# A gated blend of segment-recurrent and dilated attention: K's prepass in rounds of 16 chunks, more resident slices, other buffers and queues

## The chip, the cores and the metric

One Trainium2 chip, one NeuronCore of it. The metric is the device time of one execution of the whole program, in microseconds (us). The engines of the core are named as the profile names them: PE multiplies matrices (PEld loads its weights), DVE and ACT work on vectors, POOL is the general engine, SP only issues DMA transfers. SP, ACT and POOL each issue their transfers in their own program order; 16 DMA engines move the bytes.

## The reference

Activations and weights are bfloat16. With x of 2048 tokens by 640:

```python
g = sigmoid((x * gate_w).sum(-1))                # one gate per token
mem = mem0                                       # 8 x 640
for s in range(64):                              # segments of 32 tokens
    h = concat([mem, x[32*s:32*s+32]])           # 40 x 640
    q, k, v = h @ Wq, h @ Wk, h @ Wv             # 32 heads x 192 = 6144 columns each
    p = softmax(mask(q @ k.T * 192**-0.5))
    o = (p @ v) @ Wo                             # 40 x 640
    mem = o[:8]                                  # carried to the next segment
    a[32*s:32*s+32] = o[8:]
# branch B: 32 heads x 20, each token sees itself and 7 more, 2 apart
q, k, v = x @ wqkv
b = softmax_over_8(q[t] . k[t - 2*w] * 20**-0.5) v[t - 2*w] @ wo
out = g * a + (1 - g) * b
```

Only the 8 memory rows of a segment depend on the segment before. What the tokens' rows need of q, k and v does not, so some of it can be prepared for all 64 segments ahead.

## The kernel before

The program runs through these stages, in this order. The times are those of the profiled execution.

**Branch B, 0 to 190 us (`part_b`).** The tokens are cut into a short block (b = 0, 112 tokens, with an input tile of its own, `xT0`) and four blocks of 484. For each block, `proj(b, n, c)` makes one of five 128-row chunks of q (n = 0) or k (n = 1): five matmuls, a cast to a tile called `bqc` or `bkc` (DVE for q, and for k from block 2 on; ACT for k of blocks 0 and 1), and a store by SP into DRAM. Four tiles rotate under each of the two names, so a cast waits until the store of the cast four places earlier has landed. `load_qk(b)` then reads q and k of the block back in the layout the scores need (`bqT`, `bkT`: eight SP loads), `make_v` makes V, `gates` makes the gate values (it needs `gw_sb`, loaded from gate_w), `scores` and `values` do the attention by groups of heads. Finished rows go through DRAM into `OTc`, and `out_tile` multiplies them by wo, puts the result into a tile `bo` beside the gate, and stores it in `bsc_dram` with POOL; four `bo` tiles rotate.

The order on PE, ACT, DVE and SP is written out by hand within a `manual_schedule`: at its start `load_qk(0)`, two entries of a list of bulk loads (`fetch(2)`: xT of block 2 and gate_w), `make_v(0)`, the first projections of block 1, `gates(0)`. Then a planner deals projections, gates, V and out tiles to the steps of (block, group of heads) by cost and due step; one bulk load is issued per step for most steps. The bulk list holds what the later stages need: resident weight slices (`wres`), Q's columns of the prepass, `zTi`. After the last block the gate values are stored to `g_dram` and read back as a tile `gZ` of 128 x 4 by 16 small SP loads.

**The prepass, 190.7 to 352 us (`prepass`).** The first eight tokens' rows of all 64 segments (`zTi`, 640 x 512) are multiplied by Wq, Wk and Wv. For Q and K the result has 48 chunks of 128 columns each: five matmuls into one of eight PSUM banks, then a cast by ACT or DVE in turn into a tile `ZS` (128 x 64 segments x up to 192 values per segment), two of which rotate. A round is the chunks that share a `ZS`: 16 for Q, 24 for K. Each Q round is stored with one transfer of 2 MB by ACT; each K round with two, one of 128 values per segment (2 MB) and one of 64 (1 MB, runs of 128 bytes), into `zpk_dram`. The weight columns come from resident slices or, where a slice is not resident, through slots `wst` (POOL loads, 256 KB each, for K). V follows: for three column parts t and four groups of 128 rows, 20 matmuls and four casts into a tile `ZV` (three rotate), stored by ACT with 4 transfers each.

Beside that SP loads weight slices of part A into the space that is free: `load_late(0)` takes slices up to a bound `LATE0` (bytes per partition) while Q runs; `load_late(1)`, after the `ZS` tiles are gone, the rest, and `load_late(2)` the last seven after V. The order of the slices is q, k, v, oa, ob (parts of Wo).

**Part A, 352 us to the end.** A first segment on its own, a loop over the segments at some 18 us each (390 to 1500), and a tail. Each segment reads its prepared row of `zpk_dram` (`load_z`, and `load_vz` on POOL into `aVz`), and part of the weights is streamed from DRAM through `wst` slots by SP in every segment. L805 is its q and k matmul, L812 ACT's cast of that. Loop and tail are not touched by the diff.

The lines that the change and the prediction speak of: 143 and 141 (casts by DVE and ACT), 252 (V of B), 225 (gates), 271 and 275 (a projection's matmul and its store), 281 (`load_qk`), 347, 361, 367 and 369 (`bo`: gate copy, matmul, DVE part, store), 467 (the `gZ` loads), 526 (slice loads), 590 (K's columns), 612 and 624 (Q/K matmul and store), 638 and 646 (V matmul and store), 743 (`load_vz`).

Of the kernel before, what the change touches and what calls it, by code (L numbers as in the profile page):

```python
# [10 lines left out]
BF = mybir.dt.bfloat16  # L11
F32 = mybir.dt.float32
I32 = mybir.dt.int32

SLOTS = 7
N_EARLY = 15
N_EARLY2 = 12
N_LAST = 7
LATE0 = 41984
STREAM = [("q", 0, 1, 1), ("k", 0, 1, 1), ("k", 0, 3, 1), ("q", 1, 1, 0), ("k", 1, 0, 0), ("k", 1, 3, 1), ("q", 2, 2,  # L20
          0), ("k", 2, 0, 1), ("k", 2, 1, 1), ("k", 2, 4, 1), ("v", 0, 3, 1), ("v", 1, 1, 0), ("v", 1, 4, 1), ("v", 2,
          0, 1), ("v", 2, 3, 0), ("oa", 3, 1), ("oa", 4, 1), ("ob", 2, 0), ("oa", 7, 0), ("oa", 11, 0), ("ob", 6, 0)]
# [71 lines left out]
class _K:  # L94
# [59 lines left out]
    def part_b(self, outer):  # L154

        nc, tc, KC, S = self.nc, self.tc, self.KC, self.S
        NQ, HALO = 121, 14
# [4 lines left out]
        g_dram = self.dram.tile([4, 32, self.NT], F32, name="g_dram")  # L162
        self.xh_dram = self.laid["xh"]
        self.gZ = self.const.tile([128, 4], F32, name="gZ")
        self.pre_columns = {}
        with ExitStack() as ctx:
# [96 lines left out]
            def proj(b, n, c):  # L263
                nq, nu, c0 = shape_of(b)
                nt = nq * nu
                o0, nn = ((c0 + HALO, nt), (c0, nt + HALO))[n]
                if c == 0:
                    qk_dram[b, n] = self.dram.tile([640, nn], BF, name=f"b{'qk'[n]}_dram{b}")
                ps = bank(F32, "ps_bqk")
                for kc in range(KC):  # L270
                    nc.tensor.matmul(ps[:, 0:nn], lhsT=wqk[n][:, c, kc, :], rhs=(xT if b else xT0)[:, kc, o0:o0 + nn],
                                     start=(kc == 0), stop=(kc == KC - 1))
                t = wk.tile([128, BQ + HALO], BF, name="b" + "qk"[n] + "c", bufs=4)
                self.evac(t[:, 0:nn], ps[:, 0:nn], "dve" if n == 0 or b > 1 else "act")
                nc.sync.dma_start(qk_dram[b, n][128 * c:128 * c + 128], t[:, 0:nn])

# [66 lines left out]
            ot_dram = {}  # L343

            def out_tile(ti, padded=False):
                bo = io.tile([128, 4, 162], BF, name="bo", bufs=4)
                nc.gpsimd.tensor_copy(bo[:, :, 160:162].bitcast(F32),
                                      self.g_sb[:, ti:ti + 1].unsqueeze(1).to_broadcast([128, 4, 1]))
                for f in range(2):
# [26 lines left out]
                    proj(0, n, c)  # L376

            def columns(p):
                self.pre_columns[p] = self.get_columns("q", p)
# [53 lines left out]
            for i, (b, g) in enumerate(steps):  # L433
                work = plans[i]
                fill(work[:1])
                scores(b, g)
                fill(work[1:])
                if i > 0:
                    values(*steps[i - 1])
                if b + 1 < nb and g == 3:  # L440
                    load_qk(b + 1)
                if b > 0 and g == 1:
                    store_ot(b - 1, 0, 8)
                if b > 0 and g == 2:
# [17 lines left out]
            fill(rest)  # L462
            nc.vector.tensor_copy(last[:, :, o0:128], OTb[(nb - 1) % 2][:, 5:8, 0:128 - o0])
            nc.sync.dma_start(g_dram[:].rearrange("u t n -> (u t) n"), self.g_sb[:])
            for n in range(4):
                for q in range(4):
                    nc.sync.dma_start(self.gZ[32 * q:32 * q + 32, n:n + 1], g_dram[:, 24:32, 4 * n + q:4 * n + q + 1])
            fetch(len(bulk))
            order.close()
            for ti in (13, 14, 15, 12):  # L470
# [105 lines left out]
        self.nc.gpsimd.dma_start(t, self.wscr[key])  # L576
        return self.view(t, key)

    def get_columns(self, m, p):

        W = {"q": self.Wq, "k": self.Wk}[m].rearrange("(c p) f -> p c f", p=128)
        out = {}
        for x in range(2):
            for kc in range(self.KC):
                if (m, p, kc) in self.res_tiles:
                    t = self.res_tiles[m, p, kc][:, 1024 * x:1024 * x + 1024]
                else:
                    t = self.slots[self.slot_at % SLOTS]
                    self.slot_at += 1
                    (self.nc.sync if m == "q" else self.nc.gpsimd).dma_start(t[:], W[:, kc, 2048 * p + 1024 * x:2048 * p + 1024 * x + 1024])  # L590
                out.setdefault(kc, []).extend(t[:, f:f + 128] for f in range(0, 1024, 128))
        return out

    def prepass(self):
# [5 lines left out]
        zTi = self.zTi  # L600
        with tc.tile_pool(name="pre_zv", bufs=3, side="right", reuse_waits="tile") as zvp:
            with tc.tile_pool(name="pre_zs", bufs=2, reuse_waits="tile") as zp:
                for m in ("q", "k"):
                    n = 16 if m == "q" else 24
                    for c in range(48):
                        if c % n == 0:
                            ZS = zp.tile([128, nseg, 192], BF, name="ZS")
                        if c % 16 == 0:
                            sls = self.pre_columns[c // 16] if m == "q" else self.get_columns(m, c // 16)
                        ps = self.pst([128, NZ], F32, name="ps_pre")  # L610
                        for kc in range(KC):
                            nc.tensor.matmul(ps[:], lhsT=sls[kc][c % 16],
                                             rhs=zTi[:, kc, :], start=(kc == 0), stop=(kc == KC - 1))
                        zc = 8 * (c % 16) if m == "q" else 16 * (c % 12) + 8 * (c // 12 % 2)
                        self.evac(ZS[:, :, zc:zc + 8], ps[:].rearrange("p (i s) -> p s i", i=8))
                        if c % n == n - 1:
                            if m == "q":
                                zs = [(256 * (c // n) + 128, 0, 128)]
                            elif c < n:
                                zs = [(0, 0, 128), (256, 128, 64)]  # L620
                            else:
                                zs = [(320, 0, 64), (512, 64, 128)]
# [8 lines left out]
            for t in range(3):  # L631
                sls = [self.v_columns(t, kc) for kc in range(KC)]
                for st in range(NZ // 128):
# [9 lines left out]
                                  "dve" if (t, st) == (2, NZ // 128 - 1) else None)  # L643
                    for k in range(2 * st, 2 * st + 2):
                        for e, R, x, n in V_PIECES[t]:
                            nc.scalar.dma_start(self.zpk_dram[:, 8 * R + k:128:32, 768 + x:768 + x + n],
                                                ZV[64 * (k % 2):64 * (k % 2) + 64, :].rearrange(
                                                    "s (j e) -> s j e", j=4)[:, :, e:e + n])

    def working_tiles(self):  # L650

# [599 lines left out]
```

## Time and profile before

| | us |
|---|---|
| median of 3 runs | 1554.81 (1549.94 to 1559.15) |
| the profiled execution | 1561.53 |
| its span | 1559.8 |
| branch B | 0 to 190.7 |
| Q and K of the prepass | 190.7 to 242.5, 242.5 to 294.3 |
| V of the prepass | 294.3 to 352.1 |
| part A | 352.1 to 1559.8 |

| engine | busy us | share of the span |
|---|---|---|
| PE | 1460.0 | 94% |
| DVE | 815.2 | 52% |
| ACT | 642.5 | 41% |
| POOL | 204.8 | 13% |

All lines below come from one execution taken by the hardware profiler. A line of the timeline names the start, the time until the end of the last instruction of the group, the engine, the line of the program, the operation with out<-in, the number of instructions, and in brackets how long the engine stood idle before it and which instruction ended that. An engine's busy share says little by itself: the share is an average over stages with different limits.

### The profile page before, as it was taken

Reading aid. Unit: us, or ns where it says so; the run is one execution under the profiler, and the core shown is the slowest. Engines: PE = TensorE matmul, PEld = TensorE weight load, DVE = VectorE, ACT = ScalarE, POOL = GpSimd, SP = SyncE. Lnnn points to the kernel's source line nnn. Section 1 sums busy time; section 2 is a strip of 40 time slices with the busy share of each in tenths; the row PEclk is TensorE's granted clock in tenths of the full one; section 3 lists DMA queues with packets and bytes.
Section 4 is the critical chain, followed back from the end, with each engine's and each line's share of the span. In section 5 each row is a group of like instructions: output and inputs, shape, how many; then the busy total and the mean of one; then the engine's idle time right before and its main releaser. Section 6 shows DMA issues by size and latency. Waiting matters only on the chain. (4 is left out here: it accounts for less than half of the span.)

```text
span 1559.8 us, 90918 instructions
## 1 busy us (share of the span) xinstructions
PE 1460.0 (94%) x36746; PEld 818.7 (52%) x36746; DVE 815.2 (52%) x2246; ACT 642.5 (41%) x1673; POOL 204.8 (13%) x432
## 2 busy tenths in 40 slices
PE   6988799996899999999999999999999999999969
PEld 3444444433555555555555555555555555555547
DVE  2787433323555555555555555556555555555510
ACT  2588422222344434443444344434443444344430
POOL 0000201100111111111111111111111111111100
PEclk8999999998999999999999999999999999999979
DMA  6788686999899999999999999999999999999980
GB/s 188 193 210 218 187 272 154 222 269 281 279 330 322 318 325 325 330 325 329 330 326 322 325 323 330 324 326 332 318 318 327 334 325 321 322 332 325 303 189 16
DMA packets 374073, 446.29 MB, mean 286 GB/s; under 512 B 132504, under 2 KB 236488, under 8 KB 374008
## 3 DMA queue, kind: packets, MB, share of 16 engines
q1 hardware_dynamic: 272632, 395.77, 77.4%
q10 hardware_dynamic: 87824, 25.14, 7.2%
q0 software_dynamic: 13552, 24.47, 5.1%
q8 instruction: 46, 0.75, 0.2%
q14 instruction: 19, 0.16, 0.0%
HBM read 407.04 MB, written 38.20 MB: 285 GB/s over the span
## 5 line engine op out<-in xcount | busy, mean ns | idle before, releaser
L812 ACT CAST aP<-psx 128x512 bf16<-128x512 f32 x128 | 68.7, 589 | 362.5 <-PE psx L805 349.4
L967 PEld LDWEIGHTS <-aP 128*32 128x32 bf16 x6144 | 163.8, 96 | 66.2 <-ACT aP L946 18.5
L903 PE MATMUL psm<-wlate_v,aHa 128*32 128x512 bf16 x2048 | 186.9, 380 | 0.3 <-issue 0.3
L805 PEld LDWEIGHTS <-aHa 128*32 128x32 bf16 x4608 | 117.5, 96 | 122.5 <-issue 21.0
L967 PE MATMUL psm<-wlate_oa,aP 128*32 128x384 bf16 x2560 | 167.7, 329 | 0.0
L827 DVE STREAM_TRANSPOSE aK<-aP 128x512 bf16<-128x512 bf16 (+1 forms) x256 | 135.0, 547 | 7.4 <-ACT aP L812 1.1
L967 PE MATMUL psm<-wst,aP 128*32 128x384 bf16 (+1 forms) x896 | 121.5, 306 | 10.7 <-DMA wst<-in_slices_dram 10.7
L805 PE MATMUL psm<-wres_q,aHa 128*32 128x512 bf16 x1280 | 118.8, 381 | 11.0 <-ACT aK L812 4.7
L967 PE MATMUL psm<-wlate_ob,aP 128*32 128x256 bf16 x2688 | 126.1, 274 | 1.2 <-issue 1.2
L824 DVE STREAM_TRANSPOSE aP<-aP 128x512 bf16<-128x512 bf16 (+1 forms) x128 | 74.1, 579 | 87.4 <-ACT aP L812 87.4
L946 DVE CAST aP<-psx 128x128 bf16<-128x128 f32 (+2 forms) x192 | 75.6, 422 | 76.8 <-PE psx L934 76.6
L903 PE MATMUL psm<-wlate_v,aHb 128*32 128x512 bf16 x1152 | 115.3, 379 | 0.0
L805 PEld LDWEIGHTS <-aHb 128*32 128x32 bf16 x3072 | 75.3, 96 | 62.9 <-issue 3.5
L805 PE MATMUL psx<-wres_k,aHa 128*32 128x512 bf16 x896 | 107.5, 381 | 0.0
L912 ACT CAST aP<-psm 128x256 bf16<-128x256 f32 (+1 forms) x192 | 85.9, 447 | 48.4 <-PE psS L857 45.9
L946 ACT CAST aP<-psS 128x384 bf16<-128x384 f32 (+2 forms) x192 | 65.3, 375 | 68.7 <-PE psx L934 50.1
L743 POOL DMA_DIRECT2D aVz<-zpk_dram x64 | 34.8, 544 | 432.9 <-PE psm L805 289.4
L805 PE MATMUL psx<-wst,aHa 128*32 128x512 bf16 x512 | 88.3, 382 | 0.9 <-DMA wst<-in_slices_dram 0.6
L805 PE MATMUL psm<-wres_q,aHb 128*32 128x512 bf16 x1024 | 79.9, 381 | 0.0
L928 PEld LDWEIGHTS <-aP 32*128 32x128 bf16 (+1 forms) x4096 | 43.7, 97 | 63.5 <-DVE aK L894 32.0
L903 PEld LDWEIGHTS <-aHa 128*32 128x32 bf16 x2304 | 54.3, 96 | 42.4 <-issue 12.0
L736 POOL DMA_DIRECT2D aK<-in_xh_dram x63 | 34.2, 542 | 322.2 <-PE psm L903 301.3
(169 smaller groups left out, 3223.2 us busy)
## 6 DMA issues: line engine op xcount, KB each, us to landing
wst<-in_slices_dram SPq DMA_DIRECT2D x960, 256.0 KB, 4.6
wst<-in_slices_dram SPq DMA_DIRECT2D x384, 192.0 KB, 3.8
aP<-zpk_dram SPq DMA_DIRECT2D x64, 192.0 KB, 4.0
zpk_dram<-ZS ACTq DMA_DIRECT2D x5, 2048.0 KB
wres_q<-in_slices_dram SPq DMA_DIRECT2D x12, 512.0 KB
aVz<-zpk_dram POOLq DMA_DIRECT2D x64, 96.0 KB, 4.4
wlate_v<-in_slices_dram SPq DMA_DIRECT2D x10, 512.0 KB
wst<-in_A_Wk_dram POOLq DMA_DIRECT2D x14, 256.0 KB, 5.0
```

The source lines that it names most:

```text
L736: nc.gpsimd.dma_start(xh, row(self.xh_dram, s))
L743: nc.gpsimd.dma_start(vz[:], row(self.zpk_dram, s)[:, 768:1152])
L805: burst([nc.tensor.matmul(pq[32 * j:32 * j + 32, :], lhsT=hT[kc], rhs=sl[j], start=(kc == 0), stop=(kc == KC - 1), tile_position=(0, 32 * ...
L812: nc.scalar.copy(st[i], pqs[i])
L824: nc.vector.transpose(P[p][:, 1:5, c0:c1, :].rearrange("p b c i -> p c b i"), x)
L827: nc.vector.transpose(KT[:, c0:c1, :].rearrange("p c k -> p (c k)"), x)
L903: burst([nc.tensor.matmul(pvs[t][32 * j:32 * j + 32, :], lhsT=hT[kc], rhs=sl[j], start=(kc == 0), stop=(kc == KC - 1), tile_position=(0, 3 ...
L912: (nc.vector.tensor_copy if t == 0 else nc.scalar.copy)(Px[t][:, cs], pvs[t][:, cs])
L928: ms.append(nc.tensor.matmul(out[:, r, t, :], lhsT=v_block(2 * h + r, t)[ks, f0 - 128 * t:f1 - 128 * t], rhs=E[ks, par, EA.start + 40 * r: ...
L946: (nc.scalar.copy, nc.vector.tensor_copy)[g](x.rearrange("p (j c q) -> p j c q", j=2, q=32), pairs[g][:, :, 0:240].rearrange("p j (c q) -> ...
L967: ms.append(nc.tensor.matmul(pso[part][32 * jj:32 * jj + 32, 0:n], lhsT=oT_slot(R // 2, j, 3 * (R % 2) + t), rhs=self.o_weights(osl, part, ...
```

## The change

- K's 48 chunks are taken in another order, in three rounds of 16, each of which fills 128 adjacent values per segment, and each `ZS` (now 128 values wide for Q and K) is stored with one transfer of 2 MB. The first round takes chunks 0 to 7 and 12 to 19, the second 8 to 11, 20 to 27 and 36 to 39, the third 28 to 35 and 40 to 47.
- The weight columns are fetched by groups of eight chunks, when the first chunk of a group comes up.
- `LATE0` goes from 41984 to 71680 bytes per partition: ten slices (v_1_3 to oa_2) go from `load_late(1)` to `load_late(0)`. The space comes from the narrower `ZS`, and from a small tile `OTl` that is moved to another pool.
- `gZ` is read with 4 loads of 32 x 4 values instead of 16 of 32 x 1, at the start of the prepass, after the bulk loads.
- The short block's ten q and k chunks get a tile each; the later blocks' `bqc` and `bkc` rotate over three buffers instead of four.
- gate_w is loaded by ACT ahead of wv, instead of by SP from the bulk list; the first `fetch` takes one entry instead of two.
- `bo` rotates over five tiles instead of four.
- Of the last V part's 16 stores, eight (those of the odd rows k) are issued by POOL instead of ACT.

```diff
-LATE0 = 41984
+LATE0 = 71680
...
-            last = [wp.tile([128, 3, 128], BF, name=f"OTl{i}") for i in range(1)][0]
...
             load_xT(0, nc.sync)
+            nc.scalar.dma_start(gw[:], self.laid["gw"].unsqueeze(2))
             nc.scalar.dma_start(wv[:], self.laid["wv"])
...
-                t = wk.tile([128, BQ + HALO], BF, name="b" + "qk"[n] + "c", bufs=4)
+                t = wk.tile([128, BQ + HALO], BF, name="b" + "qk"[n] + "c", bufs=3) if b else \
+                    fw.tile([128, 128], BF, name=f"b0{n}{c}")
...
-                bo = io.tile([128, 4, 162], BF, name="bo", bufs=4)
+                bo = io.tile([128, 4, 162], BF, name="bo", bufs=5)
...
-            bulk = [(load_xT, 2, nc.sync), (dma, gw[:], self.laid["gw"].unsqueeze(2)), (load_xT, 3, nc.sync), (dma, woc[:], self.laid["wo"])]
+            bulk = [(load_xT, 2, nc.sync), (load_xT, 3, nc.sync), (dma, woc[:], self.laid["wo"])]
...
-            fetch(2)
+            fetch(1)
...
+                    last = zi.tile([128, 3, 128], BF, name="OTl")
...
-            for n in range(4):
-                for q in range(4):
-                    nc.sync.dma_start(self.gZ[32 * q:32 * q + 32, n:n + 1], g_dram[:, 24:32, 4 * n + q:4 * n + q + 1])
...
-    def get_columns(self, m, p):
+    def get_columns(self, m, h):
...
+        p, x = h // 2, h % 2
...
+                (self.nc.sync if m == "q" else self.nc.gpsimd).dma_start(t[:], W[:, kc, 1024 * h:1024 * h + 1024])
+            out[kc] = [t[:, f:f + 128] for f in range(0, 1024, 128)]
...
+                self.load_gates()
                 for m in ("q", "k"):
-                    n = 16 if m == "q" else 24
-                    for c in range(48):
-                        if c % n == 0:
-                            ZS = zp.tile([128, nseg, 192], BF, name="ZS")
-                        if c % 16 == 0:
-                            sls = self.pre_columns[c // 16] if m == "q" else self.get_columns(m, c // 16)
+                    place = [8 * c if m == "q" else 192 * (c // 24) + 16 * (c % 12) + 8 * (c // 12 % 2) for c in range(48)]
+                    for i, c in enumerate(sorted(range(48), key=lambda c: (place[c] // 128, c))):
+                        g, zc = place[c] // 128, place[c] % 128
+                        if i % 16 == 0:
+                            ZS = zp.tile([128, nseg, 128], BF, name="ZS")
+                        if (m, c // 8) not in self.pre_columns:
+                            self.pre_columns[m, c // 8] = self.get_columns(m, c // 8)
+                        sls = self.pre_columns[m, c // 8]
...
-                            for z0, f, w in zs:
-                                nc.scalar.dma_start(self.zpk_dram[:, :, z0:z0 + w].rearrange("s p f -> p s f"),
-                                                    ZS[:, :, f:f + w])
+                        if i % 16 == 15:
+                            z0 = 256 * g + (128 if m == "q" else 0)
+                            nc.scalar.dma_start(self.zpk_dram[:, :, z0:z0 + 128].rearrange("s p f -> p s f"), ZS[:])
...
-                            nc.scalar.dma_start(self.zpk_dram[:, 8 * R + k:128:32, 768 + x:768 + x + n],
+                            (nc.gpsimd if t == 2 and k % 2 else nc.scalar).dma_start(self.zpk_dram[:, 8 * R + k:128:32, 768 + x:768 + x + n],
...
+    def load_gates(self):
+        for q in range(4):
+            self.nc.sync.dma_start(self.gZ[32 * q:32 * q + 32, :], self.g_dram[:, 24:32, q::4])
```

More of the change, by code (lines that the diff above doesn't have):

```diff
@@ L161, in part_b @@
         self.oz_dram = [self.dram.tile([S // 32, 128, 192], BF, name=f"oz_dram{h}") for h in range(2)]
-        g_dram = self.dram.tile([4, 32, self.NT], F32, name="g_dram")
+        self.g_dram = g_dram = self.dram.tile([4, 32, self.NT], F32, name="g_dram")
         self.xh_dram = self.laid["xh"]
@@ L378, in columns @@
             def columns(p):
-                self.pre_columns[p] = self.get_columns("q", p)
+                for h in (2 * p, 2 * p + 1):
+                    self.pre_columns["q", h] = self.get_columns("q", h)
             def dma(*a):
                 nc.sync.dma_start(*a)
-            bulk = [(load_xT, 2, nc.sync), (dma, gw[:], self.laid["gw"].unsqueeze(2)), (load_xT, 3, nc.sync), (dma, woc[:], self.laid["wo"])]
+            bulk = [(load_xT, 2, nc.sync), (load_xT, 3, nc.sync), (dma, woc[:], self.laid["wo"])]
             bulk += [(self.load_early, k) for k in self.early]
@@ L577, in get_slice @@
         return self.view(t, key)
-    def get_columns(self, m, p):
+    def get_columns(self, m, h):
         W = {"q": self.Wq, "k": self.Wk}[m].rearrange("(c p) f -> p c f", p=128)
+        p, x = h // 2, h % 2
         out = {}
[L583 to L591, printed above, removed]
+        for kc in range(self.KC):
+            if (m, p, kc) in self.res_tiles:
+                t = self.res_tiles[m, p, kc][:, 1024 * x:1024 * x + 1024]
+            else:
+                t = self.slots[self.slot_at % SLOTS]
+                self.slot_at += 1
+                (self.nc.sync if m == "q" else self.nc.gpsimd).dma_start(t[:], W[:, kc, 1024 * h:1024 * h + 1024])
+            out[kc] = [t[:, f:f + 128] for f in range(0, 1024, 128)]
         return out
@@ L610, in prepass @@
                         ps = self.pst([128, NZ], F32, name="ps_pre")
                         for kc in range(KC):
-                            nc.tensor.matmul(ps[:], lhsT=sls[kc][c % 16],
+                            nc.tensor.matmul(ps[:], lhsT=sls[kc][c % 8],
                                              rhs=zTi[:, kc, :], start=(kc == 0), stop=(kc == KC - 1))
-                        zc = 8 * (c % 16) if m == "q" else 16 * (c % 12) + 8 * (c // 12 % 2)
                         self.evac(ZS[:, :, zc:zc + 8], ps[:].rearrange("p (i s) -> p s i", i=8))
[L616 to L622, printed above, removed]
-                            for z0, f, w in zs:
-                                nc.scalar.dma_start(self.zpk_dram[:, :, z0:z0 + w].rearrange("s p f -> p s f"),
-                                                    ZS[:, :, f:f + w])
+                        if i % 16 == 15:
+                            z0 = 256 * g + (128 if m == "q" else 0)
+                            nc.scalar.dma_start(self.zpk_dram[:, :, z0:z0 + 128].rearrange("s p f -> p s f"), ZS[:])
```

## The prediction

> **What bounds the kernel now.** I read the stretches first (busy time of each engine by stage), since the page's averages (PE 94%, DMA 0.9) hide where PE waits. The edit touches only what runs before about 390 us; the loop behind it is 94 to 98% PE.
>
> ```profile
> core 0: us, PE busy (x) PEld busy (x) DVE busy (x) ACT busy (x) POOL busy (x), PEclk, DMA share, GB/s
> 190.70:242.50 51.80, 51.80 (x241) 23.48 (x242) 15.90 (x23) 14.07 (x24) 3.25 (x6) 1.00 0.81 253
> 242.50:294.30 51.80, 51.80 (x242) 23.48 (x241) 16.59 (x24) 13.87 (x24) 6.76 (x13) 1.00 0.82 188
> 294.30:352.10 57.80, 53.93 (x241) 23.74 (x239) 16.09 (x31) 12.11 (x22) 7.96 (x38) 0.97 0.96 259
> 352.10:390.00 37.90, 24.69 (x569) 13.75 (x572) 12.04 (x34) 8.09 (x24) 2.73 (x5) 0.82 0.90 280
> ```
>
> The rows are Q, K, V and the first segment of A. Q and K each take 51.80 us for 240 matmuls and PE never idles: 0.216 us each. Nothing done to K's stores can shorten K itself. V has the same 240 matmuls and takes 57.80, so 6.0 are lost; A's first segment has PE busy for 24.69 of 37.90. Next I read PE's timeline in branch B and in these two stretches (start, duration, engine, line, operation; in brackets the idle time before it and what ended it):
>
> ```profile
> 16.42 5.04 PE L252 MATMUL ps_bv<-wv_sb,xT 128*63 128x320 bf16 x20 [3.54 <-DVE bqc L143]
> 25.88 0.65 PE L225 MATMUL ps_g<-gw_sb,xT 128*128 128x1 bf16 x20 [2.24 <-DMA gw_sb<-in_gw_dram]
> 27.50 0.26 PE L295 MATMUL ps_bS<-bqT,bkT 20*63 20x56 bf16 x8
> 178.53 0.80 PE L361 MATMUL ps_bo<-wo_sb,OTc 128*128 128x320 bf16 x4 [2.10 <-DVE bo L367]
> 321.14 4.22 PE L638 MATMUL ps_pre<-wlate_v,zTi 128*128 128x512 bf16 x11 [3.21 <-DVE ZV L143]
> 354.20 0.40 PE L805 MATMUL psx<-wres_q,aHa 128*32 128x512 bf16 x4 [2.08 <-DVE ZV L143]
> 365.11 0.62 PE L805 MATMUL psm<-wres_q,aHa 128*32 128x512 bf16 x8 [4.72 <-ACT aK L812]
> ```
>
> Last, the timelines of DVE, ACT and the issuing queues, for who was late behind these (a queue's row runs from its first issue to the end of its last, waits between them included):
>
> ```profile
> 16.09 0.28 DVE L143 CAST bqc<-ps_bqk 128x112 bf16<-128x112 f32 x1 [4.96 <-DMA bq_dram<-bqc]
> 58.21 0.68 DVE L143 CAST bkc<-ps_bqk 128x498 bf16<-128x498 f32 x1 [1.80 <-DMA bk_dram<-bkc]
> 320.40 1.29 DVE L143 CAST ZV<-ps_pre 128x512 bf16<-128x512 f32 x2 [6.83 <-DMA zpk_dram<-ZV]
> 354.09 9.36 ACTq L646 DMA_DIRECT2D zpk_dram<-ZV  x8
> 363.49 1.07 ACT L812 CAST aP<-psx 128x512 bf16<-128x512 f32 x2 [13.04 <-DMA zpk_dram<-ZV]
> 366.62 0.56 POOL L743 DMA_DIRECT2D aVz<-zpk_dram  x1 [50.38 <-DMA wst<-in_slices_dram]
> 177.10 10.55 SPq L467 DMA_DIRECT2D gZ<-g_dram  x16
> 192.33 117.08 SPq L526 DMA_DIRECT2D wlate_v<-in_slices_dram  x15
> ```
>
> **The change, part by part.**
>
> **Own buffers for the short block, and gate_w earlier (start).** The fifth q chunk's cast waited 4.96 for a buffer, until the first chunk's store (issued 8.61) had landed. That held PE 3.54; the 20 ps_bv matmuls behind ran at a granted clock of 0.50 and took 5.04, where warm ones take 1.53 for ten, so 1.98 more. gate_w's load, issued at 21.69 behind eight bqT/bkT loads and one xT load, cost 2.24. Together 7.8. Not all of it can come: the scores at 27.50 need bkT. SP issued its loads from 17.94 to 21.05, after the last q and k stores (16.39, 16.96). SP is in order; the k store before these went at 15.71 though its cast was done at 12.4, held there by the xT load ahead of it, whose completion count it shares; and the last q store shares one with the first, so it still waits for that landing near 16. bkT so lands no earlier. gate_w's landing took 4.2 (21.69 to 25.88); bkT, with such a time, would be there by 25, with 2 us by 23: the gain is 2.5 to 4.5 before PE meets the next wait, 1 if the following xT landing bites too. I take 4.0, range 1 to 5.5.
>
> **Three bqc/bkc buffers for the later blocks, not four (a new wait).** In block 2 the fifth k cast waited at 58.21 for the store of the first (cast end 47.66, store issued 48.04): about 10.5 from cast to free buffer. With three the fourth cast (54.43) meets that landing: DVE waits 3.8. Behind it in DVE's order stand the q casts, the mask multiplies (bP, L304) and the OT casts, and PE's matmuls into ps_bqk and ps_bv wait for those. Of the 3.8, 1.8 was paid before, and the fifth cast now trails by a cast and a matmul group (about 1): +3.0 of DVE, of which PE has no cover, as DVE is 91 to 95% busy in 70 to 90. In blocks 3 and 4 a cast starts 8.7 to 11.4 after the end of the one three before (75.96 to 84.66, 103.95 to 115.39), so at 10.5 it is 0 to 1.8 late; in block 1 6.5 to 10.8, where DMA is at 0.65 and landings should be shorter: 0. I take -3.0 in all; range -8 to 0.
>
> **bo with five buffers.** POOL's copies wait for the landing of a store four tiles earlier: from 165 to 187 one round is 2.2 to 4.9 (mean 3.05), and PE lost 2.10+0.59+0.62+0.32+0.71 = 4.3 between 176.4 and 190.7. One buffer more takes away one round, 3.05; PSUM and the last DVE copy remain. I take +2.5, range 0 to 4.
>
> **Gate values in 4 loads, moved behind the wres_k loads.** 12 issues fewer of 0.66 on SP (10.55/16). Behind them stood the wres_k loads, wanted after 242 and issued by 190.5, so 50 us cover them. PE has nothing of it: 0. Uncovered it would be 10.55.
>
> **K in rounds of 16 chunks.** Four store issues on ACT (2 + 2 per round of 24) become three of 2 MB; PE's 240 matmuls stay. ACT's store at 269.75 held it for 6.10 and PE lost nothing, thanks to eight PSUM banks (8 x 1.08 = 8.6 us): so 0 there. The weights are now fetched by group of eight chunks: 14 loads of 256 KB on POOL as before. The tightest: the buffer released after the 36th chunk is wanted in the 41st, 5.9 us later; these loads landed after 2.9 to 7.0 (median 4.5). Stall 0 to 1.3; I take -0.5. The first Q cast now also waits for the last bo stores (memory reuse), 3 to 4 us late: under the 8.6 of the banks, 0; with no banks it would be 4.
>
> **Ten more resident slices during K (LATE0).** v_1_3 to oa_2, 31.7 KB per partition, 4.06 MB, sat in the row "192.33 117.08": SP stood behind ZS landings three times (to 255, 286, 307), and 312 to 329 carried them with the oa slices, while DMA was at 1.02 to 1.04. In the new order these ten need no ZS memory and go out from 193 to about 215, in Q, where DMA is 0.81 and PE bound. So 300 to 330 loses some 2.9 MB (7.7 us at the 376 GB/s of 310 to 320) and one ZS store (about 10 us of DMA). A ZV buffer must be free 3 x 4.32 = 13 us after it was filled; the late landings cost 3.21, 0.66 at 313, and 1.8 by the 11 slow matmuls behind (4.22 for 11 x 0.216, granted clock 0.83 over 320 to 330). Of the 6.0 I take +4.5, range 2 to 6; if no store lands earlier 0.
>
> **Half of the last V tile's stores on POOL.** The 13.04 us wait of ACT's first cast of A is ACT's own queue: eight ZV stores took 9.36, until 363.45. With four it is free near 358.8 (4 x 1.17), before PE wants the cast (360.4). PE's 4.72 goes, and with it some of the slow clock behind it (0.83 in 360 to 370). POOL is idle from 316 to 366. Its price for a 256-run store is not in the trace: 0.54 for 128-run ones as the low bound, 3.05 (a round of bo with its landing) as the high. Two per ZV, each 4.32 apart: kept up at 0.54, and late by 2 x 3.05 - 4.32 = 1.8 per pair at the high one. aVz stands behind them on POOL: issued at 366.62, wanted at 372.65, so 6.0 of slack less the 9 by which PE comes earlier, against stores that end about 8 earlier (V's 4.5 and half the queue): near the low end it holds. Then the wait of 6.26 at 376.12 (PE for wst) moves along, but DMA is 0.81 to 0.95 there and may keep up to 2.5. I take +4.5 - 0.5 = +4.0; range 0 to 6.
>
> On this part the Trainium skill speaks against: "DMA: Bandwidth & Descriptors", section "Issuing engines are not separate DMA queues", says that transfers started by any engine share the same 16 DMA engines, and a second issuer saves only issue time, usually small. By it the 4.0 would be near 0 and the sum 4.0 smaller; here issue time itself (9.36) is what ACT's cast stood behind, so I go by the row.
>
> **Sum.** 4.0 - 3.0 + 2.5 - 0.5 + 4.5 + 4.0 = 11.5 less. The profiled execution is 1561.5 (span 1559.8 + 1.7 outside): it would be 1550.0. It lies 6.7 above the median of 1554.81; the same 11.5 off the median gives **1543.3**.
>
> **Rivals.**
> 1. *The transfers are the bound, not the waits.* The stores and slices of 290 to 390 fill 16 DMA engines whoever issues them and whenever: DMA 0.90 to 0.96 in V and A. Then V keeps half its loss and A's gain reappears at wst (376): 11.5 - 2.3 - 4.0 = 5.2, 1549.6. For it: the 6.26 wait. Against: 4 MB do leave this stretch. The skill's rule above belongs here. Chance 0.20.
> 2. *Three buffers bite in every block (slower).* If a buffer is free only 13 us after its cast (10.5 plus the 2.2 by which SP issued the store of the cast that ended at 103.95 late), casts are 13 - 6.8 = 6.2 late in blocks 1 and 2, 13 - 8.7 = 4.3 in 3 and 4: 21, and each late cast holds the next store and the bqT/bkT loads behind it, about 1 more per block: 25, against the other gains of 14.5. That is 1554.8 + 10.5 = 1565. It decides from 5.6 us of PE per block on for a slowdown over 0.5%. For it: SP's late stores at 104 to 121 and DMA at 0.92 to 0.98. Against: with four buffers only one cast of forty waited. Chance 0.13.
> 3. *It does not do what it says:* the slices still stand behind a ZS landing or an older buffer, V keeps its 6.0: 11.5 - 4.5 = 7.0, 1547.8. Against: their only waits in the new order are earlier loads. Chance 0.09.
>
> **How the numbers follow.** The forecast has 0.58. A measurement here can tell 0.5%, 7.8 us: faster means below 1547.0, slower above 1562.6. The forecast's own range is 1536 to 1547 (its terms' bounds, not all at one end). Rival 1 is just outside (a third of it faster), rival 3 half, rival 2 slower with a tenth inside the bound: faster 0.58 x 0.98 + 0.07 + 0.04 = 0.67, same 0.21, slower 0.12. The range goes from 1535 to 1560, which leaves out rival 2 and little else.
>
> **What would show it.** Start: scores(0,0) at 22 to 25 instead of 27.50, no bqc wait before. Three buffers: DVE waits for bkc stores of 3 to 4 near 54, and none over 2 elsewhere. V: 52 to 54 us long without ZV waits over 1. A: ACT's first L812 cast before 360, no L805 idle of 4.72. K: 51.8 to 53. Wrong if B ends later than 190.7, if K's PE idles over 2, or if the first loop segments start at the old time though V ended early.

## The result and the profile after

The change made the kernel slower: 1565.95 us median of 13 runs (1558.56 to 1573.73) against 1554.89 for the kernel before, run beside it 13 times (1546.91 to 1559.15). The ratio is 1.0077, 95% interval 1.0052 to 1.0102, so 11 us more where 11.5 less had been forecast. Run again on another chip the changed kernel gave 1.0080 (1.0062 to 1.0099). The profiled execution took 1573.73, its span 1572.1.

First the stretches of the changed kernel that answer to Q, K, V and A's first segment before (columns as before: PE, weight loads, DVE, ACT, POOL busy, granted clock, DMA share, GB/s):

```profile
200.60:252.50 51.90, 51.82 (x229) 23.02 (x230) 15.15 (x23) 13.18 (x23) 3.25 (x6) 0.95 0.90 283
252.50:308.40 55.90, 54.55 (x254) 24.56 (x253) 17.30 (x25) 14.76 (x26) 6.77 (x13) 1.00 0.67 169
308.40:366.80 58.40, 53.85 (x241) 23.65 (x239) 16.07 (x31) 12.50 (x22) 10.37 (x42) 0.97 0.83 200
366.80:405.00 38.20, 22.85 (x533) 12.79 (x532) 11.46 (x33) 7.63 (x22) 5.08 (x9) 0.78 0.83 265
```

Q begins at 200.68 instead of 190.68; Q and K together take 107.7 instead of 103.6; V takes 58.4 against 57.8, although DMA has fallen there from 0.96 to 0.83, as the moved slices should make it. So the loss lies in branch B first, and no stage is shorter by what had been forecast for it. PE's timeline says where:

```profile
24.72 0.21 PE L296 MATMUL ps_bS<-bqT,bkT 20*63 20x56 bf16 x1 [2.47 <-DMA bkT<-bk_dram]
59.11 1.40 PE L271 MATMUL ps_bqk<-xT,wk_sb 128*128 128x498 bf16 x3 [3.86 <-DVE bkc L143]
186.81 1.33 PE L362 MATMUL ps_bo<-wo_sb,OTc 128*128 128x320 bf16 x4 [2.80 <-ACT bo L366]
200.68 0.61 PE L615 MATMUL ps_pre<-zTi,wres_q 128*128 128x512 bf16 x1 [0.80 <-DVE bo L368]
300.60 0.82 PE L615 MATMUL ps_pre<-zTi,wst 128*128 128x512 bf16 x3 [1.35 <-DMA wst<-in_A_Wk_dram]
336.08 4.42 PE L633 MATMUL ps_pre<-wlate_v,zTi 128*128 128x512 bf16 x13 [4.36 <-DVE ZV L143]
392.85 0.21 PE L933 MATMUL psS<-aK,aVz 32*128 32x32 bf16 x2 [10.27 <-DMA aVz<-zpk_dram]
```

Each old wait is either there still (V's 3.21 is now 4.36, and 186.81 with 2.80 stands where 178.53 had 2.10) or has a successor (bkT's 2.47 at the start, and ACT's 4.72 at A's start became 10.27 for aVz); 59.11 and 300.60 are new. DVE's timeline shows who was late at 59 and at 336, and a second new wait of the first kind, for a q chunk of block 4:

```profile
58.38 0.68 DVE L143 CAST bkc<-ps_bqk 128x498 bf16<-128x498 f32 x1 [4.69 <-DMA bk_dram<-bkc]
120.44 0.66 DVE L143 CAST bqc<-ps_bqk 128x484 bf16<-128x484 f32 x1 [4.28 <-DMA bq_dram<-bqc]
335.33 1.29 DVE L143 CAST ZV<-ps_pre 128x512 bf16<-128x512 f32 x2 [8.57 <-DMA aHb<-in_xh_dram]
```

The row at 335.33 names a load of aHb that ended at that moment; ACT's cast into the same tile, at 335.27, waited 4.40 for the ZV stores (`zpk_dram<-ZV`).

For 186.81 the views are SP's queue and POOL's gate copy into the next bo, in the changed kernel:

```profile
179.90 2.85 SPq L526 DMA_DIRECT2D wres_k<-in_slices_dram  x5
184.38 2.83 SPq L647 DMA_DIRECT2D gZ<-g_dram  x4
186.12 0.19 POOL L348 COPY bo<-g_sb 128x4 f32<-128x4 f32 x1 [5.60 <-DMA bsc_dram<-bo]
```

and the stretches of 5 us at B's end, of the changed kernel:

```profile
180.00:185.00 5.00, 3.48 (x22) 1.67 (x20) 1.37 (x4) 0.00 (x0) 0.53 (x1) 1.00 1.02 339
185.00:190.00 5.00, 3.19 (x11) 1.18 (x10) 0.55 (x1) 0.53 (x1) 0.73 (x2) 0.54 0.82 296
190.00:195.00 5.00, 4.77 (x17) 1.78 (x17) 0.55 (x1) 1.06 (x2) 1.54 (x5) 0.50 0.10 34
195.00:200.00 5.00, 4.88 (x17) 1.76 (x15) 0.55 (x1) 0.53 (x1) 2.28 (x5) 0.50 0.47 166
```

and of the kernel before:

```profile
180.00:185.00 5.00, 3.79 (x23) 1.78 (x21) 1.10 (x2) 1.06 (x2) 1.29 (x4) 1.00 0.12 33
185.00:190.00 5.00, 4.65 (x27) 2.09 (x25) 0.55 (x1) 1.06 (x2) 2.68 (x7) 1.00 0.56 138
```

The five wres_k loads (three of 256 KB and two of 512) used to go out from 187.69, behind the 16 gate loads, for which SP had itself waited 4.6 (until 177.10) for the landing of g_dram's store. Now they go out at 179.90 and fill the DMA engines (1.02 against 0.12) just when the bo stores should land. POOL's copy waits 5.60 for such a landing (1.85 to 2.47 from 177 to 184 before), PE waits for bo, and then it runs the remaining out tiles, and in this execution Q's start too, at a granted clock of 0.50. Last, POOL's queue with the last five of its eight ZV stores and aVz's load behind them:

```profile
365.79 0.59 POOL L641 DMA_DIRECT2D zpk_dram<-ZV  x1 [2.59 <-issue]
371.76 0.58 POOL L641 DMA_DIRECT2D zpk_dram<-ZV  x1 [5.38 <-issue]
375.69 0.59 POOL L641 DMA_DIRECT2D zpk_dram<-ZV  x1 [3.35 <-issue]
382.40 0.58 POOL L641 DMA_DIRECT2D zpk_dram<-ZV  x1 [6.12 <-DVE aK L893]
385.59 0.59 POOL L641 DMA_DIRECT2D zpk_dram<-ZV  x1 [2.61 <-issue]
389.06 0.58 POOL L742 DMA_DIRECT2D aVz<-zpk_dram  x1 [2.88 <-DMA zpk_dram<-ZV]
```

An issue counts 0.58, but the next follows 3.2 to 6.7 later. For four of these five stores the profile shows nothing that they waited for (one came behind DVE); the first three of the eight, 2.4 to 3.2 apart, waited for the casts into ZV. So 0.58 was not the price of such a store.

### The profile page after: what moved, and what is told of

It reads as the page before. It is cut to its first block, busy times and chain, and to the rows that moved or that the text cites. A ratio compares the mean times of both kernels' runs of the same rounds, so it can differ in the third digit from the quotient of the medians.

```text
span 1572.1 us, 90901 instructions
## 1 busy us (share of the span) xinstructions
PE 1469.9 (94%) x36746; PEld 825.6 (53%) x36746; DVE 815.9 (52%) x2246; ACT 642.9 (41%) x1673; POOL 209.9 (13%) x440
## 5 line engine op out<-in xcount | busy, mean ns | idle before, releaser
L804 PEld LDWEIGHTS <-aHb 128*32 128x32 bf16 x3072 | 76.2, 96 | 61.4 <-issue 1.9
```

Source lines behind the costliest of these rows:

```text
L804: burst([nc.tensor.matmul(pq[32 * j:32 * j + 32, :], lhsT=hT[kc], rhs=sl[j], start=(kc == 0), stop=(kc == KC - 1), tile_position=(0, 32 * ...
```

## The experiments

All ratios are to the kernel before on the same chip, with their 95% interval. The marks are from each profiled execution: PE's first matmul of Q, of V and of A, and POOL's load of aK from xh (L736) in the second segment.

| kernel | Q starts | Q and K | V to A | A to second segment | ratio |
|---|---|---|---|---|---|
| before | 190.7 | 103.6 | 59.9 | 46.7 | 1 |
| changed | 200.7 | 107.7 | 60.5 | 53.0 | 1.0077 (1.0052 to 1.0102) |
| changed, again | 200.8 | 105.1 | 60.7 | 49.8 | 1.0080 (1.0062 to 1.0099) |
| changed, ZV stores on ACT | 199.4 | 105.2 | 61.7 | 47.7 | 1.0093 (1.0066 to 1.0120) |
| changed, 16 gate loads in the old place | 190.8 | 109.5 | 61.3 | 52.6 | 1.0081 (1.0055 to 1.0107) |
| changed, four bqc and bkc, four bo | 194.2 | 105.2 | 60.5 | 47.8 | 1.0096 (1.0067 to 1.0125) |
| changed, 4 gate loads in the old place | 195.3 | 106.9 | 61.5 | 50.0 | 1.0088 (1.0056 to 1.0119) |
| these three undone | 188.8 | 105.2 | 61.4 | 44.0 | 1.0006 (0.9981 to 1.0032) |
| before with the gate loads moved | 197.6 | 103.6 | 59.8 | 46.7 | 1.0036 (1.0016 to 1.0056) |
| before with ZV stores on POOL | 188.7 | 103.6 | 59.8 | 49.6 | 1.0039 (1.0017 to 1.0061) |
| before with three bqc and bkc | 195.4 | 103.6 | 60.0 | 42.6 | 1.0043 (1.0019 to 1.0066) |
| three undone, bound 41984 | 189.0 | 105.2 | 59.9 | 42.4 | 0.9992 (0.9976 to 1.0008) |
| that, four ZV tiles | 190.8 | 105.1 | 59.6 | 48.0 | 0.9996 (0.9981 to 1.0012) |
| three undone, ZV stores on SP | 190.5 | 105.2 | 60.3 | 44.3 | 1.0002 (0.9983 to 1.0021) |
| three undone, four ZV tiles, bound 68000 | 187.9 | 105.1 | 55.1 | 45.6 | 0.9971 (0.9954 to 0.9988) |
| that, ZV stores on SP | 189.4 | 105.1 | 55.2 | 45.6 | 0.9961 (0.9942 to 0.9980) |

The loop scatters from execution to execution: from the load in the second segment to the end of the span these profiles take 1147.9 to 1159.0, so a single time says little here. The marks of the prologue (all that runs ahead of that load) say more, though they scatter too: A to the second segment is 42.4 to 48.0 among the kernels whose stores all are on ACT.

**The changed kernel again.** No edit.

> The changed kernel itself beside the others on one chip. Theory (a fixed loss in the prologue): ratio to before 1.006 to 1.010, Q's first matmul 8 to 11 later than before (190.7), V's length 59.5 to 61.5, aVz waited for 8 to 13. Rival (the loss is in the loop and the prologue's lag varies by chance): the prologue's marks differ from the first profile by more than 4 us while the time does not.

Q starts 0.1 from the first profile, and aVz was waited for 10.45. The second segment came 5 earlier than in the first, so the marks do scatter by more than the 4 that the rival names. But the load there stands at 421.9 and 416.5, against 400.9 before, and from it to the end the two took 1150.2 and 1153.5, against 1159.0. The loss is in the prologue.

**ZV stores back on ACT.**

```diff
-(nc.gpsimd if t == 2 and k % 2 else nc.scalar).dma_start(
+nc.scalar.dma_start(
```

> The changed kernel with all ZV stores back on ACT. Theory (POOL makes the descriptors of a 256-run store slowly: in the changed kernel its eight stores start 2.4 to 6.7 us apart and the last at 385.59, DMA is at 0.28 in 385 to 390, and PE waits 10.27 for aVz): that wait disappears, ACT's eight stores hold its first cast of A again (a wait of 4 to 5 at L804), and the second segment starts 5 to 7 us earlier after V's end: 1566 - 6 = 1560. Rival (the 16 DMA engines are full, whoever issues): the last ZV store lands as late as before, aVz is waited for 8 to 11 us: 1566. Second rival (the loop gives a late start back): the second segment comes 6 earlier but the time moves by less than 3: 1563 to 1566.

The wait for aVz went, and ACT's came back at 7.32 (4 to 5 expected). The time did not fall: 1.0093, of four runs.

**The 16 gate loads back.**

```diff
+            for n in range(4):
+                for q in range(4):
+                    nc.sync.dma_start(self.gZ[32 * q:32 * q + 32, n:n + 1], g_dram[:, 24:32, 4 * n + q:4 * n + q + 1])
             fetch(len(bulk))
...
-                self.load_gates()
```

> The changed kernel with the 16 gate-value loads back in their old place ahead of the last weight loads of branch B. Theory (the 10.55 us that SP spent on them kept the wres_k loads off the DMA engines while the bo stores landed; without them DMA went from 0.12 to 1.02 in 180 to 185, bo stores landed 4 to 6 late, PE idled 2.80 and ran Q's start at a granted clock of 0.50): DMA in 180 to 187 below 0.6, no PE idle over 2.2 among the last out tiles, clock 1.00 there, Q's first matmul 3 to 4 earlier and V's first about 6 earlier: 1566 - 6 = 1560. Rival (five bo buffers or the late B cause it): the idle of 2.8 and the half clock stay: 1566.

Q started at 190.84, 10 earlier, no idle over 1.22 among the last out tiles, clock 1.00, DMA 0.16 in 180 to 185. V came 8 earlier (6 expected); 4 of Q's 10 were lost within Q: there the first ZS cast came 10.7 after Q's first matmul, more than eight PSUM banks hold, and PE idled 2.48. That cast waits for the last bo stores, whose memory ZS takes (DVE's first ZS cast waited 10.79 for `bsc_dram<-bo`); the last was issued at 195.68, with DMA at 1.00 to 1.04 from 194 to 200. The time did not fall here either: 1.0081, of five runs.

**Four bqc, bkc and bo buffers**, the short block's own ones gone (all share one space).

```diff
-                t = wk.tile([128, BQ + HALO], BF, name="b" + "qk"[n] + "c", bufs=3) if b else \
-                    fw.tile([128, 128], BF, name=f"b0{n}{c}")
+                t = wk.tile([128, BQ + HALO], BF, name="b" + "qk"[n] + "c", bufs=4)
...
-                bo = io.tile([128, 4, 162], BF, name="bo", bufs=5)
+                bo = io.tile([128, 4, 162], BF, name="bo", bufs=4)
```

> The changed kernel with four rotating bqc and bkc buffers for all blocks, none of its own for the short block, and four bo buffers (all three trade the same space). Theory (three buffers cost what the profile shows: DVE waited 4.69 at 58.38 and PE 3.86 at 59.11, and B runs 6.6 late from 128 on): B back to the old pace, 0.3 to 2 lost at the start again, 6 gained by 128 us: 1560. Rival (what B loses is made good further on, as Q waits for loads): Q starts no earlier: 1566.

PE's idle near 59 was 0.87 instead of 3.86, Q 6.5 earlier. The start lost more than expected (PE waited 5.67 for bqc), and the idle at the last out tiles (4.30) stayed, as the gate loads were still moved. Nor did the time fall: 1.0096, of four runs. So none of the three, undone alone, brought the 6 us that each theory had.

**The three undone together.**

> These three undone together; of the change remain K in rounds of 16, the ten slices moved to Q, gate_w early. Theory: the three parts are the whole loss, and what remains does next to nothing (K idles 1.35, V took 58.4 against 57.8 although 4 MB left it): 1553 to 1558, as before the change. Rival (each part's loss adds up and the rest is a gain that they hid): 1566 - 18.6 = 1547. Second rival (K's rounds or the moved slices cost, too): above 1560.

1.0006 (0.9981 to 1.0032), of ten runs: the three are the whole loss, within that interval. The idle times of PE that remain in this kernel's prepass and A:

```profile
286.18 0.82 PE L616 MATMUL ps_pre<-zTi,wst 128*128 128x512 bf16 x3 [1.39 <-DMA wst<-in_A_Wk_dram]
321.65 5.30 PE L634 MATMUL ps_pre<-wlate_v,zTi 128*128 128x512 bf16 x13 [4.33 <-DVE ZV L143]
364.14 1.04 PE L805 MATMUL psm<-wres_q,aHa 128*32 128x512 bf16 x8 [4.29 <-ACT aK L812]
```

K's 1.4 and V's 4.3 are there without the three, so they belong to K's order or the slices.

**Each of the three alone, on the kernel before.** The edits are the change's own lines; for the buffers only bufs=4 to bufs=3.

> The kernel before with one part of the change alone: 4 gate-value loads, issued after the last weight loads of B. Theory (SP's 10.55 us held the wres_k loads back; without them they load on top of the bo stores): PE idle of 4 to 5 among the last out tiles, half clock behind it, Q's first matmul at 194 to 199 instead of 190.7, time 4 to 8 higher (ratio 1.003 to 1.005). Rival (it takes the late B of the three buffers to make it hurt): Q within 1 of 190.7, ratio within 0.001 of 1.

> The kernel before with one part alone: half of the last V tile's stores on POOL. Theory (POOL needs 2.4 to 6.7 us from one such store to the next): aVz issued after 375 instead of 366.6, PE waits 8 to 13 for it and no longer 4.7 for ACT nor 6.3 for wst; second segment 1 to 5 later after A's first matmul than the 46.65 of before; time 1 to 4 higher. Rival (the late aVz belongs to the late start): no wait for aVz over 3, second segment earlier, time 2 to 4 lower.

> The kernel before with one part alone: three rotating bqc and bkc buffers for all blocks, no own ones for the short block. Theory (a chunk's buffer comes free some 10.5 us after its cast): DVE waits near 58 for 4 to 5 instead of 1.8, PE idles 3 to 4 there, B about 5 later by 128 us, something more at the start (short block's fourth and fifth chunk wait): Q at 195 to 198 and time 5 to 8 higher. Rival (PE makes it good before Q): Q within 2 of 190.7.

All three are slower, as the theories had it, with 12 runs each, though not in every number: POOL's stores cost more than the 1 to 4 expected, with aVz issued at 372.63 and not after 375. The gate loads alone, then POOL's stores alone, then the buffers alone (PE's timelines):

```profile
181.56 1.33 PE L361 MATMUL ps_bo<-wo_sb,OTc 128*128 128x320 bf16 x4 [4.78 <-DVE bo L367]
197.58 0.39 PE L611 MATMUL ps_pre<-zTi,wres_q 128*128 128x512 bf16 x1 [0.71 <-DVE bo L367]
```

```profile
377.99 0.21 PE L934 MATMUL psS<-aK,aVz 32*128 32x32 bf16 x2 [13.51 <-DMA aVz<-zpk_dram]
```

```profile
60.13 1.21 PE L271 MATMUL ps_bqk<-xT,wk_sb 128*128 128x498 bf16 x5 [3.07 <-DVE bkc L143]
```

Each has its wait at the place expected: for bo, with the half clock behind it until 195 (Q begins 16 us after that row), for aVz, and for the cast into bkc, for which DVE waited 3.90. The gate loads cost 0.36% of some 1550, 5.6 us; POOL's stores 6.0; three buffers 6.7. Their sum, 18.3, is more than the 11 or so between the changed kernel and the three undone. With some 3 us of uncertainty on each that alone is no contradiction, but the runs with one part undone say more. If the prices added up, taking one away would leave a ratio near 1.004; the three runs have 1.0081 to 1.0096, with 1.0055 the lowest end of their intervals. So any two of the parts cost about as much as all three, and the losses overlap. Where is open but for one place: with the 16 gate loads back, 4 of the 10 us gained were lost again at the first ZS cast.

**Four gate loads in the old place.** `self.load_gates()` goes ahead of `fetch(len(bulk))`.

> The changed kernel with the 4 gate-value loads in the old place, ahead of the last weight loads of B. Theory (what matters is that SP stands there, for the landing of g_dram's store (5 us) and the issues behind it, not their number): the wres_k loads go out some 7 later than in the changed kernel, no PE idle over 2.5 at the last out tiles, Q's first matmul at 191 to 194, time about as with the 16 loads back. Rival (it takes the whole 10.55): idle of 4 or more, half clock, Q at 198 or later.

Between theory and rival: SP sent the wres_k loads at 183.89 (179.90 changed, 187.69 before), one idle of 2.94 with a half clock remained, Q at 195.3. So what counts is when these loads go out, by degrees; the number of gate loads matters, as far as these runs show, only through that. The time, 1.0088 of seven runs, tells nothing of it.

**The bound of the early slices back at 41984**, with the three undone.

```diff
-LATE0 = 71680
+LATE0 = 41984
```

> The kernel with the three parts undone, and the bound of the early slices back at 41984 (ten slices load after the ZS tiles again); K in rounds of 16 stays. Theory (moving 4 MB to Q bought nothing, since what V waits for is the first stores of ZV held behind the last ZS store, and the ZV tile behind them): V again 59 to 62 from its first matmul to A's first, the time within 2 us of the three undone. Rival (the moved slices do help V): V 3 or more longer and the time 3 or more higher. K's idle of 1.4 stays, if it belongs to the order of the chunks; if it goes, it belonged to the slices.

V 59.9 against 61.4 with the 4 MB moved, and no difference in time (0.9992 against 1.0006, intervals overlapping): moving them bought nothing by itself that could be measured. K's idle of 1.38 stayed, so it belongs to the chunks' order.

**Four ZV tiles at that bound.**

```diff
-N_LAST = 7
+N_LAST = 8
...
-        with tc.tile_pool(name="pre_zv", bufs=3, side="right", reuse_waits="tile") as zvp:
+        with tc.tile_pool(name="pre_zv", bufs=4, side="right", reuse_waits="tile") as zvp:
```

> As the run with the bound at 41984, with four ZV tiles instead of three (one slice more is loaded after V for the space). Theory (V's loss is the wait for a free ZV tile: 4.3 and a half clock behind it): V 54 to 57 long instead of 60, the time 3 to 5 lower than with three tiles. Rival (the transfers themselves are the bound in 300 to 340): the wait moves to a later tile, V stays at 59 or more. Second rival (A's first segment hands the gain back at its wst wait): V shorter but the second segment no earlier by more than 2.

The first rival held: PE's wait moved to a later tile (2.39 at 334), V 59.6, time the same. With 4 MB more on DMA (1.01 to 1.06 in 310 to 335) the stores land late for longer than one more tile covers.

**Half of the last ZV stores on SP**, with the three undone.

```diff
-nc.scalar.dma_start(
+(nc.sync if t == 2 and k % 2 else nc.scalar).dma_start(
```

> The kernel with the three parts undone, and half of the last V tile's stores on SP instead of ACT (the changed kernel put them on POOL). Theory (what ACT's first cast of A waits for is ACT's own eight issues of 1.17; what hurt on POOL is POOL's slow making of descriptors, not the sharing): the idle of 4.3 at L805 goes below 1, no wait for aVz over 2, the second segment 2 to 5 earlier after V's end, time 2 to 4 lower. Rival (SP's own loads for A, queued behind the stores, come late): the idle reappears at the first wst, second segment no earlier, time the same or higher.

ACT's wait of 4.29 went, and one for wst of 3.18 came at 363: the rival. No gain, and unlike POOL's no loss.

**Four ZV tiles and the moved slices together.** As with four tiles, but `LATE0 = 68000`.

> The kernel with the three parts undone (moved slices and rounds of 16 stay), the bound at 68000 for space, four ZV tiles instead of three, one slice more after V. Theory (with the 4 MB gone the DMA engines are at 0.5 to 0.7 from 325 on, and what is left of V's loss is one wait for the tile of three before, filled while the last ZS store and the remaining slices land): V from its first matmul to A's first 55 to 58 instead of 59.9 to 61.4, no half clock in it; time 2 to 5 lower than before the change. Rival (the stores' own pace is the bound, whatever the tiles): the wait comes one tile later, V 59 or more, time as before. Second rival (A's first segment gives it back at wst): V shorter, second segment after A's first matmul 3 to 5 later, time as before.

Here V falls to 55.1, at full clock. PE's timeline:

```profile
319.88 1.08 PE L634 MATMUL ps_pre<-wlate_v,zTi 128*128 128x512 bf16 x3 [0.61 <-ACT ZV L141]
348.07 0.40 PE L805 MATMUL psx<-wres_q,aHa 128*32 128x512 bf16 x4 [2.08 <-DVE ZV L143]
```

and V's stretch up to its last matmul:

```profile
293.00:346.00 53.00, 52.27 (x241) 23.32 (x239) 16.09 (x31) 12.01 (x22) 7.96 (x38) 1.00 0.89 220
```

The wait of 4.33 is 0.61, and A did not hand it back (45.6). This kernel is faster than the one before: 0.9971 (0.9954 to 0.9988), 1543.45 median. Against the kernels with the slices or the tile alone the marks are clear, but the intervals of the ratios overlap a little.

**The same with half of the last stores on SP.**

> The same with half of the last V tile's stores on SP. Theory: V as in the run without it, and A's first segment as in the run with the stores on SP (no ACT wait, a wst wait of 3 in its place): time within 2 of the other. Rival (with V's stall gone the ACT queue's stores are what ends last): 3 or more lower.

0.9961 (0.9942 to 0.9980), medians 0.2 apart: as the theory, no difference that can be measured.

## Why the prediction was wrong

The forecast was a gain of 11.5; it was a loss of 11. Two terms of the sum failed outright, the gate loads (put at 0) and POOL's stores (put at a gain); the three buffers cost more than was taken for them, and three forecast gains did not show in the time. Term by term:

- *Gate values in 4 loads: forecast 0, alone a loss of 5.6.* This is the step that failed in kind. "50 us cover them" asked only whether wres_k would come in time, not what these 1.8 MB hit when they come sooner: 8 us in the changed kernel, 15 in the kernel before with the gate loads alone moved (172.58), where SP's wait of 4.6 for g_dram's store goes from ahead of them as well as the 10.55. The trace of before had DMA at 0.12 in 180 to 185 and the bo copies waiting for landings: a slow queue had kept the engines clear for what PE waited for.
- *Half of the last ZV stores on POOL: forecast +4.0 (0 to 6), alone a loss of 6.0.* ACT's wait went as forecast. The high bound for POOL's price, 3.05 per store from the bo round, was too low: stores with nothing to wait for started 3.2 to 6.7 apart, and aVz's load behind them on that queue went out at 389.06. The slack of 6.0 counted there belonged to a queue that kept up. The six kernels with these stores on POOL have 47.8 to 53.0 from A to the second segment (mean 50.5), the eight with all on ACT 42.4 to 48.0 (mean 45.5).
- *Three bqc and bkc buffers: forecast -3.0 (-8 to 0), alone a loss of 6.7.* The mechanism and the place in block 2 were right (DVE waited 4.69 at 58.38, 3.8 forecast); the term was too small. The changed kernel's B was 5.1 late behind it (66.79 against 61.66). Then block 4 has the wait too: the cast at 120.44 waited 4.28, some 13 after the end of the cast three before (106.70), where the term had 10.5 and 0 to 1.8 late; B was 6.6 late at 127.50. Every profile with three buffers has this second wait, of 2.9 to 4.3, and none with four. In the run with the buffers alone block 2 cost 3.2 (casts into bkc 1.4 late at 48.33, 4.6 at 81.60) and block 4 another 1.7; the first 1.4 arose at the start, where that run, unlike the changed kernel, lets the short block rotate three buffers too, and where the profiles scatter by as much. Rival 2 asked for such waits in every block and had 1565, near the measured time, but blocks 1 and 3 have none. That it came near is luck: other parts made up the rest.
- *Ten more resident slices: forecast +4.5, measured 0.* DMA did fall as worked out. But the slices were one of two limits on V: with them gone, the stall sat on one ZV tile, filled (by the order of the queues; this was not tried apart) while the last ZS store and the 3 MB of slices that remained were landing. The tile alone gave nothing (59.6), the slices alone nothing (61.4), both 55.1: a gain of 4.8 to 6.3 on 59.9 and 61.4, about the forecast term.
- *Start: forecast +4.0 (1 to 5.5), measured about 0* at the second scores (32.28, and 33.23 in the second profile, against 32.58). The bqc and gate_w waits went, and PE met bkT, as foreseen, but later than by 23 to 25: SP's bqT loads began at 20.27 instead of 17.94, since a k store waited until 18.10 (15.71 before) for loads that landed later; then three projections ran at half clock. That gate_w's load, now ahead of wv, made them late is likely but was not tried alone.
- *bo with five buffers: forecast +2.5, nothing to be seen.* The idle times from the first wait at the last out tiles to Q add up to 3.45 with five (the 16 loads back) and 4.20 and 3.34 with four (three undone; bound 41984).
- *K: forecast -0.5, measured -1.4*, in every kernel with the new order and in none with the old. The first ZS cast's wait, put at 0 under eight banks, is 7.6 in the changed kernel (208.29 against 200.68), close to the 8.6 that they hold, and broke through at 10.7 in the run with the 16 gate loads back.

The page of the Trainium skill weighed in the prediction ("DMA: Bandwidth & Descriptors", section "Issuing engines are not separate DMA queues") had said that a second issuer saves little. The runs bear that out: with the stores on SP the time was the same in both pairs (1.0002 against 1.0006, 0.9961 against 0.9971).

## What to carry to other kernels

When an issue that seems idle overhead goes away, look at what stands behind it in the queue and at what the DMA engines are serving at the new time: a slow issuer can be the spacing that keeps a critical store's landing short. Price a store that moves to another engine's queue by the time from one such issue to the next, not by its busy time, and by what is queued behind it. And where a stage has two limits, taking away one moves nothing; try them together before either is dropped.

## What the runs showed of the hardware

- POOL's issues of the ZV stores (256 separate pieces each) show 0.58 to 0.62 busy, close to the 0.54 to 0.57 of its loads, but followed each other at 3.2 to 6.7 in the changed kernel when their data were there. ACT's and SP's of the same shape followed at 0.6 where nothing held them (1.21 for two on ACT, 1.22 to 1.29 for two on SP). Full DMA engines alone do not explain it: DMA was at 0.72 in 380 to 385 and 0.28 in 385 to 390.
- Behind the wait for bo the granted clock was 0.50 for very different times: from 185.5 to 205.5 in the first profile of the changed kernel, with PE busy 12.84 of the 13.20 us from 186.80 to 200; for 10 us in its second profile (until 196.4, so that Q ran at full clock); for 14 with the gate loads alone and for 6 with four buffers, on the same last out tiles. The Trainium skill ("TensorE: Matmul & The Clock Gate", section "What's actually happening") gives about 3.4 us of sustained work as enough for the full clock. Here such out tiles, groups of three and four matmuls of 320 columns, did not bring it back in those 13 us, and did in 5 in the run with four buffers; what decides it is not shown. In the first profile it came back 5 us into Q's unbroken matmuls.
